# Merged 64-row units first, 128-row blocks for all head pairs in turn, and bias groups spread one a unit, in a fused attention and two-layer gated MLP kernel

## The chip, the core and the metric

The kernel runs on one core of a Trainium2 chip. Its engines run side by side, each through its own list of instructions in order: TensorE (PE; its weight loads are shown as PEld), VectorE (DVE), ScalarE (ACT), GpSimd (POOL), and SyncE (SP), which here only issues transfers between HBM and the core's memory SBUF. They wait for one another through semaphores. Matmul results land in PSUM, which POOL doesn't read here. The metric is the device time of one execution in microseconds (us), lower is better; three runs are taken.

## What is computed

Attention with a positional bias made by a small network, and then two gated layers. Cut to what matters:

```python
scores = q @ k^T / sqrt(64)                    # batch 2, 8 heads, 576 rows, head dim 64, fp32
x = log1p(|i - j|) / log1p(max(i, 1))
bias = relu(x * w1 + b1) @ w2                  # 32 hidden units, one bias per head
attn = softmax(scores + bias); y = attn @ v    # then heads side by side: 1152 x 512
z = (sigmoid(y @ Wg) * (y @ Wv)) @ Wo          # 512 -> 1536 -> 512
z = rmsnorm(z); out = (silu(z @ Wg2) * (z @ Wv2)) @ Wo2
```

## The kernel before

**Bias.** The bias of 16 rows (a *group* T, 36 in all, T = row / 16) is made in three steps that lie one step of the loop apart. `bias_h` (line 182) writes four tiles `ht`, each a relu of the table `w1l`, split over DVE, ACT and POOL by the table `BIAS_H`; `bias_mm` (line 200) multiplies them on PE (`bps`) and ACT, for four groups DVE too, copies the result to a tile `be`; `bias_end` (line 227) mirrors one side of `be` (on ACT for the first 16 groups, on POOL for the others) and SP stores it to HBM (`bias_d`). `GORDER` is the order of the groups. Sixteen groups (`PRE`) are made ahead of all attention, two a unit in units 0 to 4, one a unit in units 8 to 17.

**Units.** Attention goes unit by unit, 40 in all. Thirty-two are one batch, one pair of heads `hp` and a block `it` of 128 rows; the last eight are the 64 rows 512 to 575 (`it == 4`) of one batch, with the two heads on the two halves of the partitions. The order is `ITS = (2, 1, 0, 3, 4)`: rows 256 to 383 first, and blocks 2, 1, 0 for head pairs 0 and 1 ahead of 2 and 3. A unit n passes through these steps: SP loads its bias `bt` (`load_bias`, one for two units, three buffers, only once all groups of its rows are stored); PE makes the scores `s` (`qk_mm`); DVE adds the bias and takes the minimum, twice (`reduce_min`, M0 and M1); ACT takes the exponentials (`expo`, X0 and X1); one unit later DVE takes the reciprocal of the sums and POOL scales `p` (`normal`; DVE does it for the first six units); three units later (`TL`) PE transposes `p` (`transp`, `tp`), ACT and DVE copy the three banks to `pt` (E0, E1, E2), PE multiplies by v (`pv`), ACT copies it to `xf` and `xh`, and POOL makes the rest `xl`. The scores have two buffers in PSUM, so PE can't begin s(n+1) before M0(n) is done.

**Order.** Nothing is scheduled by a tool: `ORDERS` (line 58) is a string a phase that says in which order the steps of one turn n are written down, and each engine runs its part of that list in order. SP too is in order: a load that waits for a store holds back all that stands behind it.

**Layers.** From unit 22 on, `advance` splits the weights, 72 pieces of 128 x 512 that come as 64-bit numbers, into a high and a low part: four steps a piece, three of them on DVE and one on DVE and POOL together, with ACT between. From turn n = 40 on the gated products run (`gate_val`, `gv`, on PE), 72 steps; the first stands ahead of the last transposes of attention, and `pace` sets how many piece steps each of them writes down, by when each piece is due.

Of the kernel before, what the change touches and what calls it, by code (L numbers as in the profile page):

```python
# [45 lines left out]
SPARE = range(12, 16)  # L46

BSTEPS = {n: 2 for n in range(5)} | {n: 1 for n in range(8, 20)}
NBIAS = 20
# [3 lines left out]
LOADR = {6: (0, 2), 7: (1, 2), 8: (0, 3), 9: (1, 3)}  # L53
LOADV = {1: (0, 0), 2: (1, 0), 3: (0, 1), 4: (1, 1), 13: (0, 2), 14: (1, 2), 15: (0, 3), 16: (1, 3)}

LASTV = {22 + i: (i % 2, i // 2) for i in range(8)}
# [9 lines left out]

def rows_of(it):
    return 128 if it < 4 else 64
# [8 lines left out]
def fused_kernel(ctx: ExitStack, tc: tile.TileContext, qk, vp, tab, pcol, invp, prm, wts, rg, out):  # L77
# [53 lines left out]

    def load_raw(b, hp):
        t = wk.tile([128, 2, S], F32, tag=f"raw{hp // 2}", name=f"raw{b}{hp}", bufs=4)
        raws[b, hp] = t
        for h in range(2):
            r = slice(h * 64, h * 64 + 64)
            nc.sync.dma_start(t[r], qk[b, hp][:, r, h].rearrange("w p s -> p w s"))
# [62 lines left out]
    def bias_mm(T):  # L200
# [26 lines left out]
    def bias_end(T):  # L227
# [8 lines left out]
        if GORDER.index(T) < MIRROR_ACT:  # L236
# [3 lines left out]
        a = (T // 8) * 128 + rows_of(T // 8) - 1 - right  # L240
        r = (T % 8) * 128
        nc.sync.dma_start(bias_d[T // 8][r : r + 128, a : a + S + 15], be)
        stored.append(T)

    GORDER = [T for it in ITS for T in range(8 * it, min(8 * it + 8, 36))]
    GORDER = GORDER[2:8] + GORDER[:2] + GORDER[8:]
# [42 lines left out]
    def feed_bias(last, wait=0):  # L289
        while ahead and ahead[0] <= last:  # L290
            it = UNITS[ahead[0]][2]
            seen = stored[: len(stored) - wait]
            if any(T not in seen for T in range(8 * it, min(8 * it + 8, 36))):
                return
# [566 lines left out]
```

## Time and profile before

| | us |
|---|---|
| three runs | 657.31, 658.17, 658.32 (median 658.17) |
| span of the profiled execution | 654.7 |
| PE busy / DVE busy / ACT busy / POOL busy in it | 641.9 / 486.9 / 354.4 / 209.6 |
| first minimum (DVE, unit 0) | 28.4 |
| start of the scores of unit 4 | 47.2 |
| first product of the layers (gv, step 0) / step 1 | 188.3 / 198.1 |

The span runs from the first to the last instruction of the profiled execution; the median of the runs is 3.5 us longer. A row of a timeline gives start, length, engine, line, operation, tiles (out<-in), shapes, how many instructions were merged into it, and in square brackets how long the engine was idle before it and what ended that. A row of the chain of waits gives start, length and the work to which the end of the execution goes back. The count of PE rows is twice that of the written fp32 matmuls for `s`, `pv` and `bps` (each is run as two), and equal to it for `tp` and `gv`.

### The profile page before, as it was taken

The numbers are of one execution on the slowest core, as the hardware profiler recorded it, in microseconds if no ns is written. First come the engines' busy times: TensorE is split into PE (matmuls) and PEld (weight loads), VectorE is DVE, ScalarE is ACT, GpSimd is POOL, SyncE is SP. The second block draws the span as 40 slices with busy tenths as digits, with TensorE's granted clock in tenths as the row PEclk, the third lists the DMA queues.
The fourth block names the chain that finished last, engine by engine and source line by source line (L and its number), as shares of the span: only waits on it lengthen the run. The fifth ranks groups of instructions, "written<-read, shape, count | busy, mean of one in ns | idle before, by whom it ended". The sixth has DMA issues, their size and how long they took to land.

```text
span 654.7 us, 11794 instructions
## 1 busy us (share of the span) xinstructions
PE 641.9 (98%) x4454; PEld 576.1 (88%) x4454; DVE 486.9 (74%) x980; ACT 354.4 (54%) x753; POOL 209.6 (32%) x237
## 2 busy tenths in 40 slices
PE   8889999999999999999999999999999999999997
PEld 4336666777779999999999999999999999999997
DVE  6889898688659987888888888787877878321322
ACT  4769888888786655445444545453545535111110
POOL 6401677566454332333323321110423423000000
PEclk9979999999999999999999999999999999999999
DMA  8875855664124333433332330220324321000111
GB/s 202 278 263 185 223 173 183 220 227 121 52 65 130 111 115 97 129 97 98 102 102 90 127 95 34 65 66 32 102 93 129 97 76 55 2 0 1 49 49 48
DMA packets 28089, 71.73 MB, mean 110 GB/s; under 512 B 3457, under 2 KB 6529, under 8 KB 28033
## 3 DMA queue, kind: packets, MB, share of 16 engines
q1 hardware_dynamic: 27168, 69.80, 34.7%
q10 hardware_dynamic: 864, 1.18, 0.5%
q8 instruction: 35, 0.57, 0.4%
q14 instruction: 22, 0.17, 0.1%
HBM read 57.72 MB, written 13.25 MB: 108 GB/s over the span
## 4 chain that ended last, share of the span: by engine, by line
PE 94%; ACT 1%; issue 0%; DVE 0%; DVEq 0%
PE gv L511 46%; PE s L312 7%; PE pv L404 7%; PE tp L384 6%; PE bps L213 4%; PE acc122a L541 1%; PE acc102b L541 1%; PE acc100b L541 1%; PE acc121b L541 1%; PE acc120b L541 1%; PE acc101b L541 1%; PE acc110b L541 1%; PE acc030b L541 1%; PE acc112b L541 1%; PE acc111b L541 1%; PE acc032b L541 1%
## 5 line engine op out<-in xcount | busy, mean ns | idle before, releaser
L488 POOL TENSOR_TENSOR ff<-ff,wr 128x512 int32<-128x512 int32 x72 | 113.3, 1574 | 250.8 <-DVE ff L487 130.8
L517 DVE TENSOR_TENSOR g<-gv,sg 128x384 f32<-128x384 f32 x72 | 40.0, 556 | 95.6 <-PE gv L511 81.6
L519 ACT ACTIVATE gh<-g 128x384 fp32r<-128x384 f32 x72 | 37.8, 525 | 101.1 <-DVE g L517 101.1
L511 PE MATMUL gv<-nh,wv 128*128 128x384 f32 x288 | 76.5, 337 | 0.0
L511 PE MATMUL gv<-xh,wh 128*128 128x384 f32 x216 | 73.2, 339 | 0.0
L511 PE MATMUL gv<-xl,wh 128*128 128x384 f32 x216 | 72.9, 337 | 0.0
L511 PE MATMUL gv<-xh,wl 128*128 128x384 f32 x216 | 72.8, 337 | 0.0
L478 DVE TENSOR_SCALAR ff<-wr 128x512 uint32<-128x512 uint32 x72 | 62.1, 863 | 0.0
L515 ACT ACTIVATE sg<-gv 128x384 f32<-128x384 f32 x72 | 34.6, 481 | 50.1 <-PE gv L511 50.0
L330 DVE CUSTOM_DVE_ANT_0 t<-s,bt 128x576 f32<-128x576 f32 x72 | 51.8, 751 | 13.4 <-PE s L312 11.3
L312 PE MATMUL s<-raw 64*128 64x288 f32 (+1 forms) x320 | 52.3, 427 | 4.9 <-issue 2.9
L351 ACT ACTIVATE p<-t,mn 128x576 f32<-128x576 f32 x72 | 55.2, 767 | 3.0 <-DVE mn L330 3.0
L404 PEld LDWEIGHTS pv<-pt,v 128*64 128x64 f32 (+1 forms) x800 | 40.2, 136 | 17.2 <-ACT pt L705 11.1
L195 DVE TENSOR_SCALAR ht<-w1l,bpc 128x304 f32<-128x304 f32 (+17 forms) x100 | 53.5, 599 | 0.0
L511 PEld LDWEIGHTS gv<-nh,wv 128*128 128x128 f32 x288 | 52.4, 188 | 0.0
L404 PE MATMUL pv<-pt,v 128*64 128x128 f32 (+2 forms) x800 | 49.6, 268 | 1.4 <-ACT pt L705 1.4
L492 ACT ACTIVATE wh<-ab 128x512 fp32r<-128x512 f32 x42 | 26.4, 630 | 45.2 <-DVE ab L491 44.7
L525 DVE TENSOR_TENSOR gl<-g,gh 128x384 fp32r<-128x384 f32 x72 | 45.3, 629 | 7.0 <-ACT gh L519 7.0
L487 DVE SCALAR_TENSOR_TENSOR ff<-wr,ff 128x512 uint32<-128x512 uint32 x72 | 49.1, 682 | 0.0
L491 DVE SCALAR_TENSOR_TENSOR ab<-ab,ff 128x512 f32<-128x512 f32 x72 | 49.1, 682 | 0.0
L511 PE MATMUL gv<-nh,wh 128*128 128x384 f32 x144 | 48.7, 338 | 0.0
L366 POOL TENSOR_SCALAR p<-p,rs 128x576 f32<-128x576 f32 x60 | 48.2, 815 | 1.4 <-DVE rs L361 1.1
(358 smaller groups left out, 1583.3 us busy)
## 6 DMA issues: line engine op xcount, KB each, us to landing
wr<-wts SPq DMA_DIRECT2D x72, 512.0 KB, 3.6
bias_d<-be SPq DMA_DIRECT2D x36, 295.5 KB, 4.5
bt<-bias_d SPq DMA_DIRECT2D x16, 576.0 KB, 4.8
raw<-qk SPq DMA_DIRECT2D x16, 288.0 KB, 6.5
v<-vp SPq DMA_DIRECT2D x8, 320.0 KB, 4.5
v<-vp SPq DMA_DIRECT2D x8, 160.0 KB, 4.7
bt<-bias_d SPq DMA_DIRECT2D x8, 144.0 KB, 3.3
out<-part SPq DMA_DIRECT2D x6, 192.0 KB, 1.9
```

What stands on the lines that cost most here:

```text
L195: nc.vector.tensor_scalar(ht, src, bpc[:, t : t + 1], 0.0, op0=ALU.add, op1=ALU.max)
L312: nc.tensor.matmul(dst, raw[r, 0, it * 128 : it * 128 + rows_of(it)], raw[r, 1, hf * 288 : hf * 288 + 288], start=True, stop=True,)
L330: nc.vector.tensor_tensor_reduce(t, sp[:, :, :288], bt[:, j].rearrange("p (a c) -> p a c", a=2), -SCALE, 3.0e38, ALU.add, ALU.min, mn[:, j ...
L351: nc.scalar.activation(p[:, j], t.rearrange("p a c -> p (a c)"), AF.Exp, bias=mn[:, j : j + 1], scale=-1.0, accum_out=sm[:, j : j + 1],)
L366: nc.gpsimd.tensor_scalar(p[:, j], p[:, j], rs[:, j : j + 1], 1.0, op0=ALU.mult, op1=ALU.mult)
L404: nc.tensor.matmul(box["ps"][j * 64 : j * 64 + 64, :n], v[:k, 2 * j if it == 4 else j, c, :], pt[:k, c, j * 64 : j * 64 + 64] if it == 4 e ...
L478: nc.vector.tensor_scalar(ff, hw, 3, 0x3FFFFFFF, op0=ALU.logical_shift_left, op1=ALU.bitwise_and)
L487: nc.vector.scalar_tensor_tensor(ff, hw, 0xC0000000, ff, op0=ALU.bitwise_and, op1=ALU.bitwise_or)
L488: nc.gpsimd.tensor_tensor(ff.bitcast(I32), ff.bitcast(I32), lw.bitcast(I32), op=ALU.add)
L491: nc.vector.scalar_tensor_tensor(ab, ab, TINY_HI, ff.bitcast(F32), op0=ALU.is_ge, op1=ALU.mult)
L511: nc.tensor.matmul(ps[:, :CH], wt[:, cs], xt[:, cc, :], start=(k == 0), stop=(k == 11))
L541: nc.tensor.matmul(dst, st_[:, m * 128 : m * 128 + 128], mv, start=(head and k == 0), stop=(last and k == 2))
```

## The change

- The blocks of rows are now 0-127, 128-255, 256-319, 320-447 and 448-575 (`BLK`). The 64-row block is no longer the last but rows 256 to 319, and a unit of it takes both batches: its two `s` tiles are the batches, the partitions hold the two heads. There are 4 such *merged* units in place of 8 narrow ones, 36 units in all. For this the raw q and k of batch 1 lie with the two heads' halves exchanged (`half`), and v of batch 1 gets a third part that is shifted by 64 rows, loaded by three small transfers.
- Order of the units: merged units of head pairs 0, 1, 2 (n = 0 to 2), rows 320-447 of pairs 0, 1, 2 (n = 3 to 8), then pair 3 (n = 9 to 11), then rows 128-255, 0-127, 448-575 for all four pairs each.
- Bias: 10 groups ahead of attention in place of 16, two a unit in units 0 and 1, one a unit in units 2 to 23. ACT makes no `ht` any more; from the 13th group on POOL makes two of four; ACT mirrors the first 12 groups and POOL the others. POOL scales `p` of every unit.
- Loads: raw q and k come one pair at a time between the groups; the bias of unit 0 is loaded after 4 stored groups in place of 8; v is loaded in units 0 to 8, whole for batch 0.
- E1 is on DVE in odd units up to 25 and in all units after that (before: from unit 20 on).
- The splitting of the weights begins at unit 28 of 36 in place of 22 of 40 (`NBIAS + LAG`).

```diff
-ITS = (2, 1, 0, 3, 4)
-BIAS_H = {k: ((), (2, 3) if k % 2 else (3,)) for k in range(16)}
-BIAS_H |= {k: ((1,), ()) if k < 26 else ((), (3,)) for k in range(16, 36)}
-NORM_DVE = range(6)
+ITS = (2, 3, 1, 0, 4)
+FIRST = 12
+BIAS_H = {k: ((), (2, 3) if k % 2 or k >= FIRST else (3,)) for k in range(36)}
-PRE = 16
-MIRROR_ACT = 16
+PRE = 10
-BSTEPS = {n: 2 for n in range(5)} | {n: 1 for n in range(8, 20)}
-NBIAS = 20
+BSTEPS = {0: 2, 1: 2} | {n: 1 for n in range(2, 26)}
+NBIAS = 26
-LOADR = {6: (0, 2), 7: (1, 2), 8: (0, 3), 9: (1, 3)}
+LOADR = {5: (0, 3), 6: (1, 3)}
+BLK = ((0, 128), (128, 128), (256, 64), (320, 128), (448, 128))
...
+    def half(b, h):
+        x = (h + b) % 2 * 64
+        return slice(x, x + 64)
...
-    GORDER = GORDER[2:8] + GORDER[:2] + GORDER[8:]
+    GORDER = GORDER[2:4] + GORDER[:2] + GORDER[4:]
...
-    BLOCKS = [(hp, it) for hps in ((0, 1), (2, 3)) for it in ITS[:3] for hp in hps]
-    BLOCKS += [(hp, it) for it in ITS[3:] for hp in range(NP)]
-    UNITS = [(b, hp, it) for hp, it in BLOCKS for b in range(B)]
+    BLOCKS = [(hp, 2) for hp in range(3)] + [(hp, 3) for hp in range(3)] + [(3, 2), (3, 3)]
+    BLOCKS += [(hp, it) for it in ITS[2:] for hp in range(NP)]
+    UNITS = [(b, hp, it) for hp, it in BLOCKS for b in (range(B) if rows_of(it) == 128 else (None,))]
...
     def qk_mm(n):
+        if b is None:
+            plan = [(x, h, sps[x][h * 64 : h * 64 + 64]) for x in range(2) for h in range(2)]
         else:
+            plan = [(b, h, sps[h]) for h in range(2)]
...
     def pv(u):
+        if b is None:
+            todo = [(x, c, j) for x in range(B) for c in range(5) for j in range(2)]
...
-    for i in range(PRE + 2):
-        bias_step(i < PRE)
+    for i in range(PRE):
+        bias_step()
...
+        if i == 5:
+            load_raw(1, 1)
+            feed_bias(1)
+            qk_mm(0)
+        if i == 7:
+            table(2)
+            load_raw(0, 2)
         if i == 9:
+            load_raw(1, 2)
+            table(3)
...
-        on_dve = (2,) if n < NBIAS or n >= NU else (1, 2)
+        on_dve = (2,) if n >= NU or (n < NBIAS and n % 2 == 0) else (1, 2)
```

What stands where now, at three places.

On SP, around the first loads of bias: in before eight groups are stored (be18 to be23, be16, be17), then the bias of units 0 and 2 is loaded, and eight more groups follow.

```order
L242 DMA bias_d2_114<-be23_246 128x591
L242 DMA bias_d2_114<-be16_263 128x591
L242 DMA bias_d2_114<-be17_280 128x591
L283 DMA bt0_306<-bias_d2_114 128x2x576
L283 DMA bt2_308<-bias_d2_114 128x2x576
L242 DMA bias_d1_113<-be8_297 128x591
```

On SP in the changed kernel, from the fourth stored group on; v00, v10 and v01 (of which L156 to L159 are the four transfers of v10) and the raw q and k of pair 2 stand here too:

```order
L252 DMA bias_d2_114<-be17_209 128x591
L145 DMA raw11_235<-qk 64x2x576 x2
L291 DMA bt0_238<-bias_d2_114 64x576 x2
L291 DMA bt1_241<-bias_d2_114 64x576 x2
L252 DMA bias_d3_115<-be20_226 128x591
L252 DMA bias_d3_115<-be21_262 128x591
L145 DMA raw02_289<-qk 64x2x576 x2
L252 DMA bias_d3_115<-be22_279 128x591
L252 DMA bias_d3_115<-be23_300 128x591
L145 DMA raw12_326<-qk 64x2x576 x2
L252 DMA bias_d3_115<-be24_317 128x591
L154 DMA v00_365<-vp 128x960
```

On SP, the rows that follow, up to the loads bt3 and bt5, the bias of the first 128-row units (3 and 4, 5 and 6):

```order
L252 DMA bias_d3_115<-be25_356 128x591
L291 DMA bt2_385<-bias_d2_114 64x576 x2
L252 DMA bias_d3_115<-be26_376 128x591
L156 DMA v10_428<-vp 128x640
L157 DMA v10_428<-vp 64x320
L158 DMA v10_428<-vp 64x256
L159 DMA v10_428<-vp 64x64
L154 DMA v01_433<-vp 128x960
L252 DMA bias_d3_115<-be27_419 128x591
L293 DMA bt3_453<-bias_d3_115 128x2x576
L293 DMA bt5_455<-bias_d3_115 128x2x576
```

The loads of raw data, which stood ahead of all stores, and those of v, which stood behind bt4, now lie between the stores and the loads of bias.

On POOL, one unit of before in which a group is made (unit 16): the rest `xl`, one `ht`, a mirror, two scalings of `p`.

```order
78 L423 TENSOR_TENSOR xl1_121<-xf110_1478,xh1_118 128x128
79 L193 TENSOR_SCALAR ht135_1488<-w1l_80,nbpc_83 128x544
80 L239 TENSOR_SCALAR be31_1418<-be31_1418 128x79
81 L366 TENSOR_SCALAR p15_1447<-p15_1447,rs15_1527 128x576 x2
82 L423 TENSOR_TENSOR xl0_120<-xf022_1554,xh0_117 128x128
```

On POOL, one such unit of the changed kernel (unit 17):

```order
115 L389 TENSOR_TENSOR xl1_121<-xf101_1602,xh1_118 128x64
116 L389 TENSOR_TENSOR xl2_122<-xf101_1602,xh2_119 128x64
117 L205 TENSOR_SCALAR ht118_1612<-w1l_80,nbpc_83 128x480
118 L205 TENSOR_SCALAR ht119_1614<-w1l_80,nbpc_83 128x480
119 L248 TENSOR_SCALAR be7_1546<-be7_1546 128x127
120 L362 TENSOR_SCALAR p17_1573<-p17_1573,rs17_1649 128x576 x2
```

A second `ht` is added to each such unit, and there are 22 of them in a row (units 2 to 23) where there were ten.

On DVE, the first step on a piece of weights (`ff0`) in before, behind the minima of unit 22 of 40:

```order
271 L330 ISA t22_0_1909,mn22_1908<-s22_0_1876,bt22_1723 128x576
272 L330 ISA mn22_1908 128x1
273 L330 ISA t22_1_1911,mn22_1908<-s22_1_1877,bt22_1723 128x576
274 L330 ISA mn22_1908 128x1
275 L478 TENSOR_SCALAR ff0_1916<-wr0_1796 128x512
```

On DVE, the same step in the changed kernel, behind the minima of unit 28 of 36:

```order
297 L332 ISA t28_0_2315,mn28_2314<-s28_0_2284,bt28_2184 128x576
298 L332 ISA mn28_2314 128x1
299 L332 ISA t28_1_2317,mn28_2314<-s28_1_2285,bt28_2184 128x576
300 L332 ISA mn28_2314 128x1
301 L478 TENSOR_SCALAR ff0_2322<-wr0_2204 128x512
```

With one step a unit, 18 were written down ahead of turn NU in before and 8 are now.

## Rows read from the trace of the kernel before

**Rows 1.** The page: busy time of each engine, and the chain by engine
```profile
PE 641.9 (98%) x4454; PEld 576.1 (88%) x4454; DVE 486.9 (74%) x980; ACT 354.4 (54%) x753; POOL 209.6 (32%) x237
PE 94%; ACT 1%; issue 0%; DVE 0%; DVEq 0%
```

**Rows 2.** Chain of waits, one 128-row unit with a bias group, one narrow unit
```profile
94.46 1.13 PE tp L384 x9
95.59 1.17 PE s L312 x8
96.76 1.24 PE pv L404 x20
98.00 0.99 PE bps L213 x8
...
179.77 0.70 PE tp L384 x5
180.47 1.12 PE s L312 x8
181.59 0.88 PE pv L404 x20
...
198.06 1.96 PE gv L511 x10
```

**Rows 3.** Timeline of PE: the scores of unit 4
```profile
47.23 1.83 PE L312 MATMUL s<-raw 64*128 64x288 f32 x8
```

**Rows 4.** Windows: busy time of each engine (x), granted TensorE clock, DMA share, GB/s
```profile
5.40:17.00 11.60, 9.81 (x73) 3.28 (x73) 11.13 (x26) 7.92 (x16) 9.13 (x15) 1.00 1.05 252
24.00:37.00 13.00, 9.40 (x70) 4.33 (x74) 10.72 (x28) 8.94 (x20) 1.78 (x3) 0.95 0.83 278
...
35.50:38.90 3.40, 3.40 (x33) 1.40 (x32) 2.51 (x7) 2.10 (x5) 0.23 (x1) 0.52 0.40 93
42.30:45.70 3.40, 3.40 (x26) 0.99 (x24) 2.49 (x7) 1.88 (x4) 0.26 (x1) 0.52 0.64 247
```

**Rows 5.** Timeline of DVE from the first ht to the first minimum
```profile
6.20 4.06 DVE L195 TENSOR_SCALAR ht<-w1l,bpc 128x304 f32<-128x304 f32 x10
...
23.59 2.77 DVE L195 TENSOR_SCALAR ht<-w1l,bpc 128x368 f32<-128x368 f32 x7
28.38 0.76 DVE L330 CUSTOM_DVE_ANT_0 t<-s,bt 128x576 f32<-128x576 f32 x1 [2.02 <-DMA bt<-bias_d]
```

**Rows 6.** The page's DMA issues: count, size of one, median us to landing
```profile
bias_d<-be SPq DMA_DIRECT2D x36, 295.5 KB, 4.5
bt<-bias_d SPq DMA_DIRECT2D x16, 576.0 KB, 4.8
raw<-qk SPq DMA_DIRECT2D x16, 288.0 KB, 6.5
```

**Rows 7.** POOL's groups from 80 to 114 us: busy, mean ns, idle
```profile
L366 POOL TENSOR_SCALAR p<-p,rs 128x576 f32<-128x576 f32 x14 | 13.1, 950 | 0.0
L193 POOL TENSOR_SCALAR ht<-w1l,nbpc 128x464 f32<-128x464 f32 (+7 forms) x8 | 5.6, 705 | 0.9
L423 POOL TENSOR_TENSOR xl<-xf,xh 128x128 fp32r<-128x128 f32 (+1 forms) x9 | 3.8, 427 | 8.0 <-ACT xh L422 8.0
L239 POOL TENSOR_SCALAR be<-be 128x159 f32<-128x159 f32 (+7 forms) x8 | 2.3, 293 | 0.7
```

**Rows 8.** DVE's ht of 576 elements: from 29 to 34 us, and from 80 to 114
```profile
L195 DVE TENSOR_SCALAR ht<-w1l,bpc 128x576 f32<-128x576 f32 x3 | 1.4, 514 | 0.0
...
L195 DVE TENSOR_SCALAR ht<-w1l,bpc 128x576 f32<-128x576 f32 x3 | 2.3, 812 | 0.0
```

**Rows 9.** Timeline of DVE around step 0 of the layers
```profile
192.78 0.56 DVE L517 TENSOR_TENSOR g<-gv,sg 128x384 f32<-128x384 f32 x1 [3.93 <-PE gv L511]
193.25 0.68 DVE L496 TENSOR_TENSOR wl<-ab,wh 128x512 fp32r<-128x512 f32 x1
...
200.02 0.69 DVE L496 TENSOR_TENSOR wl<-ab,wh 128x512 fp32r<-128x512 f32 x1
```

More of the change, by code (lines that the diff above doesn't have):

```diff
@@ L64, with groups_of @@
 TINY_HI = 1.125 * 2.0**-15
+BLK = ((0, 128), (128, 128), (256, 64), (320, 128), (448, 128))
 def rows_of(it):
-    return 128 if it < 4 else 64
+    return BLK[it][1]
+def groups_of(it):
+    a, r = BLK[it]
+    return range(a // 16, (a + r) // 16)
+IT_OF = {T: it for it in range(5) for T in groups_of(it)}
 def bias_width(it):
@@ L135, in load_raw @@
         for h in range(2):
-            r = slice(h * 64, h * 64 + 64)
+            r = half(b, h)
             nc.sync.dma_start(t[r], qk[b, hp][:, r, h].rearrange("w p s -> p w s"))
@@ L283, in load_bias @@
                 nc.sync.dma_start(bt, rows[:, : 2 * w].rearrange("i (a k) -> i a k", a=2)[:, :, :S])
-        st[n, "bt"] = st[n + 1, "bt"] = bt
-    ahead = list(range(0, NU, B))
+        st[n, "bt"] = bt
+        if b is not None:
+            st[n + 1, "bt"] = bt
+    ahead = [n for n in range(NU) if UNITS[n][0] != 1]
     def feed_bias(last, wait=0):
@@ L342, in expo @@
     def expo(n, j):
-        if j >= jobs(n):
-            return
         if j == 0:
@@ L393, in pv, with one @@
         pt = pts.pop(u)
-        v = vs[b, hp]
-        n = rows_of(it)
+        r0, n = BLK[it]
         box = {}
-        def step(c):
+        if b is None:
+            todo = [(x, c, j) for x in range(B) for c in range(5) for j in range(2)]
+        else:
+            todo = [(b, c, j) for c in range(5) for j in range(2)]
+        k = len(todo) // 5
+        def one(x, c, j):
+            v = vs[x, hp]
+            if b is None:
+                at, w, m = x * 64, (2 * j if x == 0 else 2 - j), pt[:, 4 * x + c, j * 64 : j * 64 + 64]
+            else:
+                at, w, m = 0, j, pt[:, 4 * j + c]
+            dst = box["ps"][j * 64 : j * 64 + 64, at : at + n]
+            nc.tensor.matmul(dst, v[:, w, c, :], m, start=(c == 0), stop=(c == 4))
@@ L399, in go, with step @@
+        def step(i):
             def go():
-                if c == 0:
+                if i == 0:
                     box["ps"] = bank(f"pv{b}{hp}{it}")
-                for j in range(2):
-                    k = 64 if it == 4 and c == 4 else 128
-                    nc.tensor.matmul(
-                        box["ps"][j * 64 : j * 64 + 64, :n],
-                        v[:k, 2 * j if it == 4 else j, c, :],
-                        pt[:k, c, j * 64 : j * 64 + 64] if it == 4 else pt[:, j * 4 + c, :n],
-                        start=(c == 0),
-                        stop=(c == 4),
-                    )
@@ L428, in step @@
+                if b is None:
+                    for x in range(B):
+                        place(xf[:, x * 64 : x * 64 + 64], x, hp, x * S + r0, n)
+                else:
+                    place(xf, b, hp, b * S + r0, n)
             return go
-        peq.extend(step(c) for c in range(5))
+        peq.extend(step(i) for i in range(5))
     def members(l, g):
```

153 lines of the change are left out of this document (63 added, 90 removed).

## The prediction

> **What bounds the kernel now.** I read the page first: PE is busy for 98% of the span, and the chain that ends last is PE for 94% [rows 1]. A busy share is an average, so the second view is the chain in order of time. From about 55 us on its pieces touch: a 128-row unit is 1.13 (transposes) + 1.17 (scores) + 1.24 (times v) = 3.54 us of PE with nothing between, and a bias group adds 0.99 [rows 2]. There a faster DVE, ACT or POOL is worth nothing; only less work on PE is. The third view is the start, where this doesn't hold: the scores of unit 4 begin only at 47.2 us [rows 3], after DVE had waited for a load of bias [rows 5] and PE had run at a lower clock [rows 4]. The layers from 198 us on [rows 2] are the same work before and after, and PE is full there. So the change can move three things: how much PE work attention has, how early PE becomes full, and whether the layers find their weights.
>
> **PE's work.** I compare what is left for PE from the scores of unit 4 to step 1 of the layers; in before this is 198.1 - 47.2 = 150.9 us, nearly all of it full. What differs:
> - The eight narrow units go: 8 x (0.70 + 1.12 + 0.88) = 21.6 us [rows 2], all in the full stretch.
> - Of the 32 full units, before has done four scores and one transposing by then, the changed kernel only the score of unit 3 (its units 0 to 2 are merged ones): 3 x 1.17 + 1.13, +4.6 us.
> - Of the merged units, still to do are two transposings (2.3), three products with v, and the whole fourth unit. No row shows a merged unit. Its transposes are nine as in a full unit, 1.13. Its v products are twice those of a narrow unit, whose 0.88 is a price for ten, part of it start-up; 0.88 to 1.76, I take 1.5. Its eight score products are twice the four of a narrow unit: 1.12 if four tiles run side by side where two do now, 2.24 if not; I take 1.7. Together 2.3 + 4.5 + 4.3 = +11.1 us, by the ends 2.3 + 2.6 + 3.1 = 8.0 and 2.3 + 5.3 + 5.1 = 12.7.
> - Bias groups left: 22 in place of 15 (14 of 36 are done at that point where 21 were). 7 x 0.99 = +6.9 us.
>
> Sum: -21.6 + 4.6 + 11.1 + 6.9 = **+1.0 us** (-2.1 to +2.6). The merging saves PE work, but the groups made later use it up; what counts is when unit 4 starts.
>
> By the Trainium skill, page TensorEngine Tiling (Array Packing), section Tiling Modes, 64x64 mode gives four independent tiles; then 1.12 holds, which takes 0.6 us off the sum. The rows here show two side by side and none with four of this shape.
>
> **When unit 4 starts.** In before the first minimum waits for the load of its bias until 28.4 us; DVE was through its 40 `ht` at 26.4 [rows 5]. With three table steps that is 20.2 us from the first, 0.50 an `ht`; ten groups need 25, so DVE is ready at 6.2 + 12.6, about 19. The bias of unit 0 waits for four stores in place of eight and lands near 21 (four raw loads, four stores, itself, at the rates below), so the first minimum is some 7 us earlier.
>
> But the next loads don't follow at that pace, as the SP order shows. The load bt3 (units 3 and 4) waits for the store of the twelfth group, and what lies ahead of it in the queue is: six raw loads in two halves, 12 x 288 KB; 12 stores of 295.5 KB; bt0 to bt2, 864 KB; bt3 itself, 576 KB [rows 6]; v for three pairs, 3 x 480 KB; the rest of the table, 160 KB. That is 3.5 MB of raw data and 6.7 MB of others. While raw loads ran (5.4 to 17 us) the queue was full, share 1.05, at 252 GB/s; from 24 to 37 us it moved 278 GB/s at a share of 0.83, so 335 when full [rows 4]. 3.5/252 + 6.7/335 = 14 + 20 = 34 us, from 5.4 to 39.5. Ahead of bt3 the queue must run empty, since it is issued only when the twelfth store has landed; a bias load takes 4.8 us to land [rows 6], of which 1.8 are its bytes. So bt3 lands at 42.5, and with a little idle time at the first loads 43.5; the scores of unit 4 follow the first minimum, **44.2 us, 3.0 earlier** than in before. PE has far less to do up to there: after the first minimum three scores, five groups and one transposing, some 10 us. The bounds: 41 if nothing but the bytes counts, 46.5 if the raw rate holds for half of the others too.
>
> **The clock.** In before PE was granted 1.2 GHz, half of full speed, in two stretches of 3.4 us, 35.5 to 38.9 and 42.3 to 45.7 (0.52 in the rows), between pieces in which it waited [rows 4]; both lie ahead of unit 4, in time that I have counted. In the changed kernel PE has little to do from 21 to 44 us, and nothing for some 5 us ahead of unit 4, so I expect such a stretch to reach into the full part: half of 3.4 is **+1.7 us** (0 to 3.4 for two).
>
> **The weights.** When step 0 of the layers is written down, 11 piece steps stand ahead of it in place of 21. DVE is stopped in before at the product of step 0 until 192.8 [rows 9]; after that the changed kernel needs 11 more steps for piece 4, which step 1 reads 14 products in, at 0.2 each [rows 2] 2.7 us after it starts. PE has 2 x 1.13 + 3 x 1.24 = 6.0 us in between and, as in before (198.1 - 192.8 - 2 x 0.70 - 3 x 0.88), 1.3 idle, so piece 4 is due 10.0 us after the product. Eight steps took 7.4 us in before, 193.25 to 200.7 [rows 9], 0.93 each with waits and 0.68 without: 11 x 0.93 + 0.5 + 0.6 for two copies = 11.3 or 8.6. **+0.7 us** (0 to 1.5). Later pieces are due at a rate that `pace` meets, with six steps a turn where it asked for five.
>
> **What costs nothing.** ACT loses its `ht` and half of E1; it is not on the path. DVE gets E1 in odd units and loses one `ht`. POOL gets a second `ht`: its unit is 2 x 0.95 (p) + 2 x 0.71 (ht) + 0.5 (xl) + 0.29 (mirror) = 4.1 us against PE's 3.54 + 0.99 = 4.5; in before it waited 8.0 us in eight units for `xh`, 1.0 each [rows 7], which covers the 0.71. That cover is thin; see below.
>
> **Sum.** -3.0 + 1.0 + 1.7 + 0.7 = +0.4 us on the profiled span of 654.7, thus 655.1; the median of the runs is 3.5 longer than the span, 658.6. I forecast no change.
>
> **Rivals.**
> - *Faster: the early transfers cost less, and the clock stays up.* Unit 4 starts at 41 (-6.2), no stretch at half clock, the merged unit at its low price: -6.2 + 1.0 - 1.0 + 0.7 = -5.5, 652.7; with half of it 655.4. For it: stores and bias loads alone ran faster than raw loads [rows 4], and PE's remaining work is sure. Against: the bytes are all needed, and bt3 stands behind v loads that unit 3 does not need.
> - *Slower: POOL becomes the bound of units 4 to 23.* It decides from the point where POOL's unit passes 4.5 us, that is, where its instructions run a tenth longer. DVE's `ht` of 576 elements took 0.514 us with POOL idle and 0.812 with POOL busy [rows 8], so the two slow each other, and POOL's scaling took 0.95 in that stretch. With 0.25 us over in each of 22 units, less the 1.5 us by which a group is ahead of its use, +4: 662.5; with 0.5, +9. For it: both engines have `ht` in every unit. Against: DVE has two `ht` where it had three, so it disturbs POOL for less time.
> - *Slower: the start and the weights together take their bad ends*, unit 4 at 46.5, two half-clock stretches, 1.5 for the weights: -0.7 + 1.0 + 3.4 + 1.5 = +5.2, 663.4; the middle of this case 661.
>
> The Trainium skill, page GPSIMD Engine Reference, section Specifications, says that POOL shares its SBUF interfaces with DVE and contends with DVE's instructions of the two-port kind or with two inputs. The two means of 0.514 and 0.812 agree; by the rule alone, every `ht` that moves to POOL is partly paid by DVE, and the second rival is the likelier.
>
> **Chances.** A measurement of this kernel can tell 0.2% from no change, 1.3 us. No change (657 to 659.5): 0.37, since the terms nearly cancel; its own range is that. Faster 0.35. Slower 0.28: 0.14 for POOL, 0.14 for start, clock and weights. The range leaves out a tenth at each end: 652.5 to 663.
>
> **What would show it.** Right: the first minimum near 21 us, the load bt3 landing at 42 to 45 and DVE idle for some 5 us until then; PE granted half clock somewhere between 30 and 48; pieces of 3.54 and 4.5 us touching from unit 5 on; POOL waiting for `xh` 0.2 to 0.4 us a unit. Wrong at the start: bt3 landing ahead of 41 or DVE not waiting for it. Wrong on POOL: its wait for `xh` gone and PE idle ahead of `bps`. Wrong on the weights: PE idle ahead of step 1 or 2 for over 2 us. Wrong on PE's work: the merged scores outside 1.1 to 2.3 us.

## The result, and the profile after

| | before | after |
|---|---|---|
| median of the runs, us | 658.25 (657.31 to 658.63, 4 runs) | 668.12 (667.03 to 669.67, 4 runs) |
| ratio after to before | | 1.0147 (95% interval 1.0126 to 1.0167) |
| span of the profiled execution, us | 654.7 | 666.3 |
| start of the scores of unit 4 | 47.2 | 50.2 |
| layers: step 0 / step 1 / step 7 | 188.2 / 198.0 / 234.0 | 195.8 / 208.3 / 245.2 |

The change makes the kernel 1.5% slower. I had forecast 658.6 with a range to 663.0; the time lies above the range. (The two spans differ by 11.6, the medians by 9.9: the execution profiled in before lies 3.5 below its median, that of the changed kernel 1.8. The working below goes by the spans.) The page of the changed kernel, first the busy times and then the chain by engine, which answer to [rows 1]:

```profile
PE 641.0 (96%) x4450; PEld 574.2 (86%) x4450; DVE 471.7 (71%) x944; ACT 343.5 (52%) x729; POOL 244.3 (37%) x289
...
PE 89%; DMA 4%; DVE 2%; ACT 2%; issue 1%; POOL 1%; SPq 0%; DVEq 0%; POOLq 0%; ACTq 0%
```

PE has as much busy time as before and 11.6 us more span: the time is in waits, and the chain holds DMA and DVE where it held PE almost alone. There are five places.

**The start.** Timelines of PE, SP (issues of transfers) and DVE of the changed kernel ahead of unit 4; the scores of unit 4 answer to [rows 3].

```profile
31.52 0.74 PE L322 MATMUL s<-raw 64*64 64x288 f32 x2 [1.86 <-DMA raw<-qk]
...
50.17 2.96 PE L322 MATMUL s<-raw 64*128 64x288 f32 x8 [8.60 <-DVE mn L332]
53.06 1.61 PE L222 MATMUL bps<-ht,prms 128*32 128x416 f32 x8
54.60 1.80 PE L375 MATMUL tp<-ident,p 128*128 128x128 f32 x9
```

```profile
37.60 0.33 SPq L252 DMA_DIRECT2D bias_d<-be  x1
...
40.24 0.58 SPq L154 DMA_DIRECT2D v<-vp  x1
40.93 0.38 SPq L252 DMA_DIRECT2D bias_d<-be  x1
45.14 0.90 SPq L293 DMA_DIRECT2D bt<-bias_d  x2
```

```profile
22.62 0.76 DVE L332 CUSTOM_DVE_ANT_0 t<-s,bt 128x576 f32<-128x576 f32 x1 [3.32 <-DMA bt<-bias_d]
...
49.34 0.76 DVE L332 CUSTOM_DVE_ANT_0 t<-s,bt 128x576 f32<-128x576 f32 x1 [9.44 <-DMA bt<-bias_d]
```

The first minimum comes at 22.6, 5.8 us earlier than in [rows 5]. But the scores of unit 2 wait for raw data until 32.6, and the products of the eleventh and twelfth group stand behind them on PE. So SP can issue the stores of these two only at 37.6 and 40.9, with five loads of v in between, which keep it until 40.8; bt3 is issued at 45.1, when the twelfth store has landed, and DVE has it at 49.3. The window of these scores and products (columns of [rows 4]):

```profile
32.00:38.00 6.00, 5.61 (x29) 1.45 (x28) 1.92 (x5) 1.37 (x3) 2.69 (x5) 0.50 0.45 169
```

The transfers' share is 0.45 there, so the queue stands half empty, and PE runs at half clock (0.50), which makes these two stores later still.

**The clock.** Windows of the changed kernel around unit 4; the columns are those of [rows 4].

```profile
47.00:50.00 3.00, 0.00 (x0) 0.00 (x0) 0.66 (x1) 0.00 (x0) 0.00 (x0) 0.50 1.01 380
50.00:53.00 3.00, 2.83 (x8) 1.80 (x8) 2.97 (x11) 2.11 (x5) 1.65 (x3) 0.50 1.05 373
...
56.00:59.00 3.00, 3.00 (x56) 2.26 (x58) 2.35 (x8) 2.03 (x7) 0.45 (x1) 1.00 0.99 259
```

PE has had no work since 41.6; 1.2 GHz is granted from about 45.6 on and lasts to 55.9. By the starts in the timeline the scores, group and transposes take 2.89, 1.54 and 1.73 where 1.17, 0.84 and 1.13 would do: 3.0 us. Not all of it is the clock: scores that begin right behind a minimum for which PE stood take 1.84 at full clock too (166.61 to 168.45, in the last block below), so I estimate the clock at 2.3 and that at 0.7.

**The units with groups 0 to 3.** The chain of waits of the changed kernel, one of four such units (columns: start, length, work), and DVE's timeline there.

```profile
80.51 1.18 PE bps L222 x16
...
83.01 1.91 PE s L322 x8
```

```profile
81.71 0.58 DVE L231 TENSOR_SCALAR be<-bps,nip,corr 128x288 f32<-128x288 f32 x1 [1.70 <-PE bps L222]
82.20 0.75 DVE L332 CUSTOM_DVE_ANT_0 t<-s,bt 128x576 f32<-128x576 f32 x1
```

In these groups DVE copies the second half of the product to `be`. PE reaches that product only behind the products with v, so DVE stands 1.7 us, and the minimum of the unit, whose scores have long been there, stands behind it; so the next scores come late. Such a unit takes 5.6 us where 1.13 + 1.17 + 1.24 [rows 2] and about 1.1 for a large group make 4.6: 1.0 too many, four times.

**The last block.** In the changed kernel the last bias group is finished in unit 25, and the first bias of rows 448 to 575, the first piece of weights and two more pieces are loaded in a row behind its store. At 164.6 PE loses 1.5 us (by the starts, transposes 1.99 for 1.13, scores 1.84 for 1.17). PE's timeline of the changed kernel:

```profile
164.62 1.20 PE L375 MATMUL tp<-ident,p 128*128 128x128 f32 x9
166.61 1.91 PE L322 MATMUL s<-raw 64*128 64x288 f32 x8 [0.78 <-DVE mn L332]
```

**The weights.** Between steps 0 and 1 of the layers PE is idle 2.2 us (12.5 less 4.28 for step 0, 2 x 1.13 and 3 x 1.24) where it was 1.4, and 0.9 more are lost up to step 7. After that nothing is: the lag stays at 11.2. PE's timeline of the changed kernel:

```profile
207.09 1.31 PE L410 MATMUL pv<-pt,v 128*64 128x128 f32 x18 [1.91 <-ACT pt L710]
...
211.04 0.44 PE L511 MATMUL gv<-xh,wh 128*128 128x384 f32 x1 [0.33 <-ACT wh L492]
```

The first wait is for a copy `pt` that stands on ACT behind a step on a piece (`wh`, 205.9 to 206.5). The second, in the thirteenth product of step 1, is for the piece itself.

The merged units themselves cost what a full unit costs: from the chain of waits, one of four products with v and the only merged scores (x16) in the full part.

```profile
66.40 1.31 PE pvNone L410 x40
...
73.88 1.13 PE s L322 x16
```

With that the lag of 11.2 at step 7 is explained, and the spans to 0.4 us:

| from before to after | us |
|---|---|
| unit 4 starts later (50.17 - 47.23) | +2.9 |
| PE work from there to step 1: -21.6 + 4.6 + 9.8 (merged) + 6.5 (groups: 22 for 20.8, before 15 for 14.3) | -0.7 |
| scores, group and transposes from unit 4 on (clock 2.3, scores behind a minimum 0.7) | +3.0 |
| units with groups 0 to 3 | +4.0 |
| last block | +1.5 |
| weights: the copy ahead of step 1, the piece in it (0.8 + 0.9) | +1.7 |
| waits of under 0.15 each | +0.3 |
| waits of before in units 4 to 6, which are gone | -1.5 |
| sum, against 11.6 measured | +11.2 |

The last line but one rests on two rows of the timeline of PE before, which take 0.45 and 0.43 more than two groups of that width and scores do:

```profile
48.99 2.43 PE L213 MATMUL bps<-ht,prms 128*32 128x496 f32 x16
...
52.48 1.67 PE L312 MATMUL s<-raw 64*128 64x288 f32 x8
```

with 0.59 in the scores of unit 4 itself, which last 1.76 up to the next start.

### The profile page after: what moved, and what is told of

Its sections match the earlier page's. It is cut to its first block, busy times and chain, and to the rows that moved or that the text cites. A ratio compares the mean times of both kernels' runs of the same rounds, so it can differ in the third digit from the quotient of the medians.

```text
span 666.3 us, 11763 instructions
## 1 busy us (share of the span) xinstructions
PE 641.0 (96%) x4450; PEld 574.2 (86%) x4450; DVE 471.7 (71%) x944; ACT 343.5 (52%) x729; POOL 244.3 (37%) x289
## 4 chain that ended last, share of the span: by engine, by line
PE 89%; DMA 4%; DVE 2%; ACT 2%; issue 1%; POOL 1%; SPq 0%; DVEq 0%; POOLq 0%; ACTq 0%
PE gv L511 45%; PE s L322 6%; PE pv L410 5%; PE tp L375 4%; PE bps L222 4%; DMA bias_d<-be 1%; DMA bt<-bias_d 1%; DMA raw<-qk 1%; ACT p L351 1%; PE pvNone L410 1%; DMA wr<-wts 1%; PE acc122a L541 1%; PE acc121b L541 1%; PE acc101b L541 1%; PE acc100b L541 1%
## 5 line engine op out<-in xcount | busy, mean ns | idle before, releaser
L488 POOL TENSOR_TENSOR ff<-ff,wr 128x512 int32<-128x512 int32 x72 | 115.1, 1599 | 260.7 <-DVE ff L487 97.7
L322 PE MATMUL s<-raw 64*128 64x288 f32 (+1 forms) x320 | 54.2, 461 | 17.9 <-DVE mn L332 10.4
L362 POOL TENSOR_SCALAR p<-p,rs 128x576 f32<-128x576 f32 x72 | 59.5, 833 | 28.6 <-DVE rs L360 26.5
L322 PEld LDWEIGHTS s<-raw 64*128 64x128 f32 (+1 forms) x320 | 28.6, 187 | 35.3 <-DVE mn L332 15.4
L515 ACT ACTIVATE sg<-gv 128x384 f32<-128x384 f32 x72 | 34.5, 480 | 45.1 <-PE gv L511 45.0
L478 DVE TENSOR_SCALAR ff<-wr 128x512 uint32<-128x512 uint32 x72 | 57.7, 802 | 0.0
L525 DVE TENSOR_TENSOR gl<-g,gh 128x384 fp32r<-128x384 f32 x72 | 48.6, 676 | 6.8 <-ACT gh L519 6.8
L375 PEld LDWEIGHTS tp<-ident,p 128*128 128x128 f32 x324 | 35.5, 142 | 17.2 <-ACT xh L388 10.0
L487 DVE SCALAR_TENSOR_TENSOR ff<-wr,ff 128x512 uint32<-128x512 uint32 x72 | 49.2, 684 | 0.0
L511 PE MATMUL gv<-nl,wh 128*128 128x384 f32 x144 | 48.6, 337 | 0.0
```

Of the source, the lines that this page charges most:

```text
L322: nc.tensor.matmul(dst[:, hf, :288], raw[r, 0, r0 : r0 + rows], raw[r, 1, cs], start=True, stop=True)
L362: nc.gpsimd.tensor_scalar(p[:, j], p[:, j], rs[:, j : j + 1], 1.0, op0=ALU.mult, op1=ALU.mult)
L375: nc.tensor.transpose(tp[:, x * 128 : x * 128 + 128], p[:, a : a + 128], ident)
L478: nc.vector.tensor_scalar(ff, hw, 3, 0x3FFFFFFF, op0=ALU.logical_shift_left, op1=ALU.bitwise_and)
L487: nc.vector.scalar_tensor_tensor(ff, hw, 0xC0000000, ff, op0=ALU.bitwise_and, op1=ALU.bitwise_or)
L488: nc.gpsimd.tensor_tensor(ff.bitcast(I32), ff.bitcast(I32), lw.bitcast(I32), op=ALU.add)
```

## Experiments

Medians; the kernel before ran beside each, at 658.3 to 659.2. My theory after the two traces: the loss is made of these separate places, above all the order of the start and the half copies on DVE. The rivals: POOL is the bound of units 4 to 23 (as in the prediction), or the bytes in the queue are.

### Half copies on ACT, in the changed kernel and in the kernel before

```diff
-BIAS_HALF_DVE = (0, 1, 2, 3)
+BIAS_HALF_DVE = ()
```

> ACT copies both halves of groups 0 to 3 to be; in the changed kernel DVE copies the second half. Theory H: the four units with these groups (80 to 101 us) take 5.6 us where their neighbours take 4.6, because DVE, in order, waits for the second bps block, which PE reaches only behind the products with v, and the minimum of the next unit stands behind that copy. Then each loses about 1.0 us and all four come back: 668.1 - 4.0 = 664.1, and the scores in these units take 1.17 in place of 1.84. Rival: a group of two blocks costs PE this by itself (two PSUM banks more); then the units stay at 5.6 and the time at 668. By a third reading ACT is full there, the copy is merely late in another place, and half comes back, 666.

Measured 664.16 (663.06 to 666.69): 4.0 less, as theory H had it. The chain there is now PE alone:

```profile
81.40 1.13 PE tp L375 x9
82.53 1.17 PE s L322 x8
```

The same edit in the kernel before:

> The kernel before with ACT copying both halves of groups 0 to 3. Theory H: DVE's half copy costs only where PE is otherwise full; in the kernel before these groups stand in the first units, where DVE and PE wait for loads anyway, so nothing comes back: 658.3, within 1 us. Rival: the half copy costs 1.0 us a group wherever it stands; then 654.3. Or ACT is the later one there (busy 9.8 of 10 us from 50 to 60): up to 2 slower.

Measured 653.18 (652.51 to 654.39), ratio 0.9928 (0.9904 to 0.9952): **theory H was wrong about the place.** I had taken the start of before for a wait for loads. PE's timeline of before with the half copies on ACT:

```profile
43.53 1.64 PE L312 MATMUL s<-raw 64*128 64x288 f32 x8
```

The scores of unit 4 begin at 43.5 in place of 47.2 [rows 3], and the page has no slice with half clock any more, so the stretches of [rows 4] went with these waits. In the kernel before, DVE's row that tells it stood in the timeline all along:

```profile
44.71 0.55 DVE L222 TENSOR_SCALAR be<-bps,nip,corr 128x264 f32<-128x264 f32 x1 [0.91 <-PE bps L213]
```

So the change did not add a cost of 4.0; it carried one over, from a start where it made unit 4 3.7 us late, to the full part. Both kernels pay it, and without it they are 11.0 us apart (664.2 and 653.2).

### The start: loads of v later, or the groups earlier

```diff
-LOADV = {0: ((0, 0),), 1: ((1, 0), (0, 1)), 2: ((1, 1),), 3: ((0, 2),), 4: ((1, 2),), 7: ((0, 3),), 8: ((1, 3),)}
+LOADV = {3: ((0, 0), (1, 0)), 4: ((0, 1), (1, 1)), 5: ((0, 2), (1, 2)), 7: ((0, 3),), 8: ((1, 3),)}
```

> The v loads of units 0 to 4 are issued two or three units later (from unit 3 on). Theory V: SP issues them one after another between 38.0 and 40.8 us, and the store of the twelfth bias group, made at about 39.2, is issued only at 40.9; so bt3 lands 1.7 us earlier, at 47.5 in place of 49.2, unit 4 starts near 48.5, and the time is 666.4, or 665.5 if the stretch at half clock gets shorter too. Rival: the group itself is made late (the scores of unit 2 wait for their raw load, the minimum of unit 2 for bt2), the v loads only fill the time; then bt3 lands at 49 and the time stays at 668. If v is then late for its first product, the time is above 668.

Measured 670.00 (668.91 to 670.44). The half about bt3 holds: unit 4 starts at 47.0, 3.2 earlier, so the loads of v between the two stores had cost more than the 1.7 us expected. But v is then late, and over 5 us are paid back: 4.1 in three waits for v, the rest at half clock behind them. Timeline of PE:

```profile
46.99 2.96 PE L322 MATMUL s<-raw 64*128 64x288 f32 x8 [5.53 <-DVE mn L332]
...
66.43 0.80 PE L410 MATMUL pvNone<-pt,v 128*64 128x64 f32 x20 [2.36 <-DMA v<-vp]
```

Thirteen steps ahead of unit 0:

```diff
-PRE = 10
-BSTEPS = {0: 2, 1: 2} | {n: 1 for n in range(2, 26)}
-NBIAS = 26
+PRE = 13
+BSTEPS = {n: 1 for n in range(25)}
+NBIAS = 25
```

> Thirteen bias steps stand ahead of unit 0 in place of ten, and then one step a unit up to unit 24 (before: two in units 0 and 1, one up to unit 25). Theory S: in the changed kernel DVE is idle for 19 us between 19 and 50 us and PE for 15, because the groups that bt3 needs stand in program order behind the scores of unit 2, which wait for a raw load until 32.6; made ahead of unit 0 they fill the idle time, their stores go out near 25 and bt3 lands near 38 to 42, so unit 4 starts 8 to 12 us earlier than at 50.2; one group less is left for the full part (-0.9) and the last block's bias is made one unit earlier (up to -1.5). 668.1 - 10 - 1.5 = 656.6, between 654 and 659. Rival: the bytes in the queue decide (by the estimate of the prediction bt3 lands at 43.5), and the later minimum of unit 0 gives part of it back; then unit 4 starts at 45 or later and the time is 662 or more.

Measured 657.46 (656.03 to 658.67), ratio to before 0.9988 (0.9968 to 1.0008): 10.7 us come back from one edit. The first minimum is 0.7 us later than with ten steps, and bt3 is issued at 36.1 in place of 45.1:

```profile
36.13 0.38 SPq L293 DMA_DIRECT2D bt<-bias_d  x1
```

```profile
37.47 0.76 DVE L332 CUSTOM_DVE_ANT_0 t<-s,bt 128x576 f32<-128x576 f32 x1 [9.44 <-DMA bt<-bias_d]
```

```profile
38.29 2.96 PE L322 MATMUL s<-raw 64*128 64x288 f32 x8 [3.52 <-DVE mn L332]
...
43.89 1.24 PE L322 MATMUL s<-raw 64*128 64x288 f32 x8
```

Unit 4 starts at 43.9 (the last line), 6.3 earlier and not 8 to 12; the rest is the half clock, which now lies on unit 3, ahead of it (3.0), a group less (0.9), and steps 0 and 1 of the layers 0.7 closer, with the pieces a unit earlier. The edit does two things at the start: the groups move ahead, and with them the five loads of v fall behind bt3. By the run above the second is worth 3.2 of the 6.3; no run has the first alone. Between 24 and 38 us the transfers' share is 0.92, so here the bytes nearly decide. Unit 4 starts where the prediction put it (44.2), but not for its reason: the last load for which DVE stands is bt2, until 37.5 (the row of DVE), and not bt3.

### POOL

```diff
-BIAS_H = {k: ((), (2, 3) if k % 2 or k >= FIRST else (3,)) for k in range(36)}
+BIAS_H = {k: ((), (2, 3) if k % 2 and k < FIRST else (3,)) for k in range(36)}
```

> From the thirteenth group on POOL makes one ht and DVE three, as in the kernel before, where the changed kernel gives each two. By the rival of the prediction (POOL's unit is what PE waits for in units 4 to 23) some 4 us come back: 664. By the trace of the changed kernel POOL waits 0.3 to 1.2 us a unit there and the pieces of PE touch, so nothing comes back: 668, or up to 2 more if DVE's third ht makes its minimum late.

Measured 668.10 (667.51 to 668.76): no change. POOL's largest wait from 80 to 114 us, first in the changed kernel, then in this one (columns: total, times, longest):

```profile
POOL xl L389 <- ACT xh L388: 4.5, 6, 1.2
```

```profile
POOL xl L389 <- ACT xh L388: 6.5, 7, 1.3
```

It had slack with two `ht` and has more with one. The rival of the prediction falls.

### The last block and the weights

Bias two units earlier:

```diff
-BSTEPS = {0: 2, 1: 2} | {n: 1 for n in range(2, 26)}
+BSTEPS = {0: 2, 1: 2, 20: 2, 21: 2} | {n: 1 for n in (*range(2, 20), 22, 23)}
```

> Units 20 and 21 make two bias groups each, so the last group is made two units earlier and the weights begin two units earlier. Theory B: the stop of PE at 164.6 (transposes 1.98 for 1.13, scores 1.84 for 1.17) is DVE waiting for the first bias of the last block, which is issued only when the last group is stored (161.2) and lands at 165.6; two units earlier it is 9 us earlier and the 1.5 us come back; two or three more piece steps then stand ahead of step 0 of the layers, worth 0 to 1: 665.6 to 666.6. Rival: DVE waits there for the first piece of weights (landed 166.9), which moves along with the bias, so the stop moves too and the time stays at 668, or 667 by the pieces.

Measured 668.57 (668.25 to 670.59): no change, though the stop at 164.6 is gone and step 1 begins 1.9 earlier. The window of steps 4 to 5 shows where it went (busy of PE first):

```profile
223.50:232.80 9.30, 6.55 (x37) 6.22 (x36) 8.22 (x13) 5.60 (x11) 2.94 (x2) 1.00 0.40 115
```

From step 4 to 5 it takes 9.3 in place of 6.3: a new wait (below). To tell bias from weights, the piece steps alone one unit later:

```diff
-LAG = 2
+LAG = 3
```

> The changed kernel with the piece steps one unit later and nothing else. At 164.6 PE loses 1.5 us, while DVE waits first for the last block's first bias (until 165.7) and then for the first piece of weights (until 167.1). Theory B: the bias is the later one for PE, and a piece step moved away saves only what lies between, at most 0.5, which the one piece step less ahead of the layers takes back: 668. Theory L: it is the piece, as it was in the kernel with thirteen steps; then the 1.5 come back: 666.6. Rival: neither, the wait is at the next bias (issued behind the pieces): slower by up to 1.

Measured 668.83 (667.02 to 670.73): no change, theory B. The chain names the bias, and the stop stays:

```profile
159.08 4.01 DMA bt<-bias_d
...
164.04 1.91 PE s L322 x8
```

Two piece steps a unit:

```diff
-            "C": lambda: n >= NBIAS + LAG and advance(EARLY if live else EARLY + MORE, 1 if live else 2),
+            "C": lambda: n >= NBIAS + LAG and advance(EARLY if live else EARLY + MORE, 2),
```

> Two piece steps a unit instead of one from unit 28 on, so some 18 to 20 stand ahead of step 0 of the layers in place of 11. Theory W: steps 0 and 1 of the layers stand 12.5 us apart where 9.8 + 1.9 (the wider transposes and products in between) would do, and 0.9 more is lost up to step 7, since pieces are late: 1.7 us come back, 666.4. Rival: what the pieces gain DVE, ACT and POOL lose in the units (POOL's add takes 1.6 us a piece), so the units stretch from 3.55 and it is 668 or slower; or the loads of pieces, one after another, set the pace, and it stays at 668.

Measured 670.58 (669.21 to 673.37): the first rival. DVE, third in the row, is busy for 27.2 of 28 us and becomes the bound (PE 25.4):

```profile
168.00:196.00 28.00, 25.36 (x248) 18.64 (x245) 27.16 (x65) 22.95 (x57) 19.26 (x25) 1.00 0.32 101
```

### The clock

Behind the transposes of unit 0, in `transp` (42 in place of 32 in the second run):

```diff
+        if n == 0:
+            more = bank("warm2")
+            for _ in range(32):
+                nc.tensor.matmul(more[:, :128], ones, ones, start=True, stop=True)
```

> Behind the transposes of unit 0 (41.5 us) PE gets 32 multiplications of ones by ones, about 6.8 us, in the time in which it waits for the scores of unit 4; they change no result. Theory C: the half clock of 45.6 to 55.9 follows from PE's idle time ahead of unit 4, so with PE busy there the scores, the bias group and the transposes take 1.2, 0.85 and 1.1 in place of 2.9, 1.5 and 1.7, and 3.0 us come back: 665.1. Rival: the half clock comes for another reason; then the added work runs at half speed too, ends behind 50 us and makes it slower, 668 to 674.

Measured 667.81 (666.77 to 668.32). PE was busy up to 49.2 and idle for 2.0 us; half clock came all the same, and scores, group and transposes took 5.4 us in place of 6.2 (3.1 at full clock). PE's timeline, and a window (columns of [rows 4]):

```profile
51.14 2.37 PE L322 MATMUL s<-raw 64*128 64x288 f32 x8 [1.98 <-DVE mn L332]
```

```profile
54.00:56.00 2.00, 2.00 (x14) 1.02 (x7) 1.70 (x7) 0.83 (x2) 1.45 (x4) 0.53 0.12 46
```

> The changed kernel with 42 multiplications of ones in PE's idle time ahead of unit 4, where the run with 32 left 2 us of idle time behind them and the half clock then came at 52 in place of 45.6 and cost 2.2 us in place of 3.1. Theory C: idle time of PE is what the half clock follows, 2 us are enough for it; with less than 1 us idle there the scores, group and transposes run in 1.2, 0.85 and 1.1: 3.0 come back, less up to 0.5 for scores that stand behind the last multiplication: 665.1 to 665.6. Rival: half clock falls due at about that time whatever PE does, then it stays between 667.5 and 669.

```profile
41.15 9.64 PE L380 MATMUL warm<-ones 128*128 128x128 f32 x84
50.73 1.24 PE L322 MATMUL s<-raw 64*128 64x288 f32 x8
```

Theory C holds in the place: without idle time the granted clock is 1.00 from 38 to 58 us and the three pieces take 3.1, 3.0 less. In the time it does not hold: 668.57 (666.96 to 669.36). In the profiled execution, the shortest of the four and 1.1 us shorter than that of the changed kernel, 0.6 went to scores that stood behind the last of the ones (bt3 was there by 49.0, 0.4 earlier than in the changed kernel) and 1.0 to a longer stop at the last block, until the first piece of weights had landed. Why the median kept nothing at all stays open.

### Mended together

Thirteen steps and the copies on ACT:

> Thirteen steps ahead of unit 0, and ACT copying both halves of groups 0 to 3. If start and half copies are two separate losses, the gains add: 4.0 us below the kernel with thirteen steps alone, so 652.6 if that one is at 656.6, which is faster than the kernel before (658.3). If the half copies' cost is only exposed because units 9 to 12 stand where they do, an earlier start changes nothing in that, and the same 4.0 hold; by the rival that ACT has no room once the start is full, 2 or less.

Measured 654.91 (651.99 to 656.23), 2.6 and not 4.0 below the thirteen steps alone; its four runs spread over 4.2 us, so differences to it are rough. The units are at 4.6, but being earlier they ran into the first piece of weights:

```profile
145.56 6.78 DMA wr<-wts
```

So the same with `LAG = 3`:

> As the kernel with thirteen steps and whole copies on ACT, and the piece steps begin one unit later (three units behind the last bias group, not two). In that kernel DVE stood 3.8 us at the first piece step, until 152.3, when the piece had landed; its load is issued behind the last block's first bias and beside two more pieces. PE lost 3.6 us by it (products with v 3.26 for 1.24, transposes, scores 2.29 for 1.17 at half clock). Theory L: one unit, 3.55 us, is what lacks, so the wait goes and 3.3 come back, less up to 0.5 for one piece step less ahead of the layers: 651.6 to 652.1. Rival: the same full queue then holds DVE at the next bias, or the one piece step less stops the layers later by as much; 654 to 655.

Measured **653.10** (652.66 to 653.64), ratio to before **0.9915** (0.9882 to 0.9948). The stop is gone; of the 3.3 us 1.8 are left in the median. Steps 0 and 1 stand 12.5 apart where it was 11.7, which is 0.9 of the 1.5 that lack. With the bias of unit 2 ahead of its raw data as well (`feed_bias(2)` ahead of `load_raw(1, 2)`):

> As the kernel with piece steps one unit later, and the bias of unit 2 is loaded ahead of the raw load of unit 2, where it is issued behind seven stores and a v load. In the kernel with thirteen steps and whole copies DVE waited 10.4 us, until 37.5, for this load, and the scores of unit 3 for DVE. Theory D: the four groups that it needs were stored by 21 us, so it can land near 31; the minimum of unit 2 then follows its scores (34.4), some 3 us earlier, and unit 4 starts at 42.5 in place of 45.4: -3 on the kernel with piece steps later, 648.6 to 649. Rival: its 295 KB only change places with the raw load and the stores behind it in a full queue (share 1.05), the scores of unit 2 come later by the same bytes and bt3 decides; then 0 to 1 come back.

Measured 652.64 (652.10 to 654.06): the rival, and within the spread of the run above. Unit 4 starts at 42.7 in place of 43.9, but its scores, group and transposes take 5.2 us in place of 3.1. With 24 multiplications of ones ahead of the scores of unit 2 on top:

> As the kernel with the bias of unit 2 loaded early, and 24 multiplications of ones, 5.1 us, on PE ahead of the scores of unit 2, in the time in which PE waits for raw data. Theory C: without the idle time there PE keeps 2.4 GHz where the kernels with thirteen steps ran the scores of units 2 and 3, two groups and the transposes at half clock (32 to 43 us); some 3 us less, 645.5 to 646. Rival: the work at half clock there is hidden by waits for loads (unit 3's minimum, bt3) and only the last pieces count: 0 to 1.5 come back; or the multiplications end behind the raw load and hold the scores: up to 1.5 slower.

Measured 655.11 (654.40 to 656.74), slower. The half clock moved and did not go:

```profile
44.31 2.96 PE L326 MATMUL s<-raw 64*128 64x288 f32 x8 [4.84 <-DVE mn L336]
```

PE now waits 4.8 us there, as DVE has bt3 only at 43.5 in place of 41.9, and pays on the scores of unit 4.

Does the merging bring anything? Two steps in units 1 and 2 each, first on the kernel of 653.1, then on that of 652.6:

```diff
-BSTEPS = {n: 1 for n in range(25)}
-NBIAS = 25
+BSTEPS = {0: 1, 1: 2, 2: 2} | {n: 1 for n in range(3, 23)}
+NBIAS = 23
```

> As the kernel with thirteen steps, whole copies on ACT and piece steps one unit later, with two steps in units 1 and 2, so that the last group is made in unit 22 and not 24. Theory G: the merging does save PE work, and what the changed kernel loses is the groups that it makes in the full part and the late weights; DVE and PE stand for some 10 and 8 us between 27 and 44 us, so two more groups cost nothing there and are missing later (2 x 0.95), and two more piece steps stand ahead of the layers (0.8 of the 1.7 that steps 0 to 2 lose): 653.1 - 2.7 = 650.4, which is also below the kernel before with whole copies on ACT (653.2). Rival: their two stores lie ahead of the load bt3 in a queue that is full (share 1.05), and unit 4 starts 1 to 2 us later: 652 to 653.5, no better than before with whole copies.

Measured 654.00 (652.83 to 656.07). Unit 4 starts at 46.4, 2.4 later, as the rival had it; but step 1 begins no later than there (192.9 and 193.1), and what is lost in the profiled execution, the longest of the seven, is lost behind it: step 5 begins 3.4 later, of which 2.75 are one wait of PE:

```profile
217.09 0.69 PE L541 MATMUL acc001a<-gh,wh 128*128 128x384 f32 x1 [2.75 <-ACT part L553]
```

> The same two steps in units 1 and 2, on the kernel in which the bias of unit 2 is loaded ahead of its raw data. Theory G: 652.6 - 2.7 = 649.9. Rival: with bt2 early DVE and PE have less idle time there (unit 4 started at 42.7), so the two groups push the minimum of units 2 and 3 by up to 2 us, and half of it is left: 651 to 652.

Measured 654.68 (654.08 to 655.34). Here step 1 begins at 190.9 in place of 193.6: the 2.7 of theory G are there, though unit 4 starts 2.0 later (44.7, now at full clock), 3.2 us ahead of the kernel before with whole copies (194.1). Step 5 begins 1.0 later all the same, by the same wait. The chain:

```profile
209.41 1.24 DVE wl L496
...
214.18 0.86 ACT part L553 x2
215.08 1.07 PE acc001a L541 x3
```

PE needs the PSUM of the first output sums, ACT and DVE empty it behind the piece steps that stand ahead, and PE waits 2.65 us. So neither theory is clean: the saving of PE work is real and reaches step 1, and this wait takes it back, here, in the run before it and with the bias two units early. No run has the saving without the wait.

## Why the prediction was wrong

- **When unit 4 starts: the step that failed first** (44.2 forecast, 50.2 measured). The sum took bytes by rates and let the queue run empty only ahead of bt3. The last two stores ahead of bt3 were not limited by bytes but by program order: their groups stand on PE behind scores that wait for a raw load until 32.6, and on SP five loads of v stand between them (3.2 us). Once the groups stand ahead of unit 0, and v behind bt3, the start is 43.9. That this is near the 44.2 is luck, since bt2 decides it there. The upper bound, 46.5, was made from rates only and so was no bound.
- **The base of the comparison** was the second failure. I read the 47.2 of before as given by loads and the 150.9 us behind it as full. It held 3.7 us of half copies ahead of unit 4 and 1.5 us of waits behind. The edit that moves groups 0 to 3 into units 9 to 12 was put at nothing: "What costs nothing" doesn't name DVE's half copies, and by the first paragraph a faster DVE is worth nothing in the full part. It is a wait of DVE for PE with the next minimum queued behind it, 4.0 us.
- **PE's work**: -0.7 for +1.0 forecast, within its bounds. The merged scores took 1.13 where I took 1.7, the products with v 1.31 for 1.5. Sixteen matmuls in the row take as long as the eight of a narrow unit (1.12 [rows 2]), so four do run side by side. The Trainium skill has it so (TensorEngine Tiling (Array Packing), section Tiling Modes).
- **The clock**: right in kind, 3.0 for 1.7 (some 2.3 of it the clock), inside its bounds. But the stretch lasted 10.3 us, 45.6 to 55.9, where I took one of 3.4.
- **The weights**: 1.7 for 0.7, just above the bound of 1.5. The wait for the piece in step 1 is the one forecast and came out at 0.9; the other 0.8 is the copy ahead of step 1, where I had kept the idle time of before.
- **The last block** (1.5) was in no step: I followed the last group to PE and to the weights, but not to the bias load that waits for its store.
- **From span to median** I added the 3.5 of before; the changed kernel's median lies 1.8 above its span.
- **Rivals.** POOL as the bound: false. Start, clock and weights at their bad ends was the right direction, at 663.4, and lacked two of the five places. *Faster* (652.7) is near the mended kernel's 653.1, by luck: unit 4 starts there at 43.9 and not 41, and half clock still falls on unit 3.

## What to carry over

When a change moves work, list for each moved instruction what stands behind it on its engine in the new place, and what held it in the old one: a wait that is hidden among others in the start of the profile is a cost in either place. A transfer that waits for a store is late by the longest chain of program order ahead of that store, and a sum of bytes is only its lower bound. Here the changed kernel with its tables mended (653.1) and the kernel before with one table mended (653.2) are equal: what looked like the effect of the change was the fit of its tables to the queues. What the merging itself is worth, with both kernels mended as far as they go, stays open.

## What the runs showed of the hardware

- A store to HBM and the load that depends on it took 8.4 us here (issue at 40.9, issue of the load at 45.1, DVE goes on at 49.3).
- Ahead of unit 4, 2.0 us without work on PE were followed by as low a clock (0.53) as 8.6 us were (0.50); 1.9 us at 207.1 of the changed kernel, and 1.9 us at 29.3 of before with the copies on ACT, were not (1.00 in both places). Work on products of ones kept 2.4 GHz (1.00), at no gain in the time.
- DVE instructions that read SBUF alone and began while POOL added ended 0.3 to 0.6 us after POOL: `wl` took 1.80 for 0.69 [rows 9], `ff` 1.06 to 1.55 for 0.41. The product `g`, one input of which is in PSUM, took its 0.55 beside such an add. Timelines of DVE and POOL in the kernel with two steps in units 1 and 2 and bt2 early:

```profile
206.21 0.55 DVE L517 TENSOR_TENSOR g<-gv,sg 128x384 f32<-128x384 f32 x1
206.68 1.06 DVE L478 TENSOR_SCALAR ff<-wr 128x512 uint32<-128x512 uint32 x1
...
209.34 1.80 DVE L496 TENSOR_TENSOR wl<-ab,wh 128x512 fp32r<-128x512 f32 x1
211.06 0.41 DVE L478 TENSOR_SCALAR ff<-wr 128x512 uint32<-128x512 uint32 x1
```

```profile
205.63 1.82 POOL L488 TENSOR_TENSOR ff<-ff,wr 128x512 int32<-128x512 int32 x1 [2.09 <-ACT wh L492]
209.08 1.51 POOL L488 TENSOR_TENSOR ff<-ff,wr 128x512 int32<-128x512 int32 x1 [1.62 <-ACT wh L492]
```

The Trainium skill names that contention (GPSIMD Engine Reference, section Specifications), and the rows agree. Its price here, DVE standing until POOL is done, is above the 0.514 to 0.812 of [rows 8].
